# An attention and gated feed-forward kernel whose planner gets a limit on transfers, new margins and a new order of the last output tiles

## The chip, the cores and the metric

The kernel runs on one core of a Trainium2 chip. The metric is device time in microseconds (us), as the median of several executions. Engines are named as the profile names them: PE is TensorE (PEld its weight loads), DVE is VectorE, ACT is ScalarE, POOL is GpSimd, and SP issues most transfers.

## The reference

The first half is attention with a band and a few sink positions, the second a gated feed-forward layer on its result (3072 tokens, width 512, 1536 hidden columns).

```python
scores = (1 / sqrt(64)) * q @ k.T           # 4 batches, 8 heads, 768 positions, 64 wide
keep = (pos_k < n_sink) | ((rel >= 0) & (rel < window))   # n_sink 4, window 128
a = softmax(where(keep, scores, -1e9))
x = (a @ v) as [3072 tokens, 512]
gate = 1 / (1 + exp(-(x @ w_gate)))
out = (gate * (x @ w_val)) @ w_out          # w_gate, w_val: 512 x 1536, w_out: 1536 x 512
```

The three weights come as 64-bit floating-point numbers, which the kernel decodes itself to 32 bits.

## The kernel before

**Order of work.** Nothing is issued where it is written. Every step becomes an operation of a `Plan` (line 254) with a priority, one or several engines it may run on with a duration for each (`ways`), and the tiles that it reads and writes. `Plan.run` then plays the program through once with these durations and writes down, engine by engine, the order in which it would start the operations; that order is what the chip executes. The constants at the top of the file are the planner's durations, margins and due times. `SLACK` and `DSLACK` are added to each hand-over between engines, `SURE` and `SURE_D` are the further time that PE wants an input to be ready for before it prefers the operation (when no operation is that sure, it takes one that is merely ready), `GAP` and `HOLD` let an engine wait for an operation that is due soon, `BACKV` is the queue on DVE from which POOL may take a DVE operation. Where PE has nothing ready in the first 130 us of the plan, `run` inserts matmuls of the identity (`warm`, `m<-ident`), called fills here, if PE was not busy enough in that stretch.

**Attention.** There are 12 pieces of 256 tokens (numbered `tn`), each with 8 heads; `attend` (line 931) plans one head `u` of one piece. PE makes the scores, DVE masks them and finds the maximum (`top`), ACT exponentiates (`exp`), the row sums are inverted, `P` is scaled (POOL, or ACT, or DVE), PE transposes `P`, ACT, DVE and POOL build the masked `wt` from it, and PE multiplies `wt` by the values. The result goes into `xf` (`X0` for the first piece). The first 20 heads (`u < PLAIN`) use plain 32-bit matmuls; later ones split operands in a high and a low part of a faster 32-bit type, whose low part (`rest`) is a subtraction on POOL or DVE.

**Weights.** `decode` (line 1269) turns a 128 x 512 block of a weight into 32 bits in four passes: ACT takes the high word (`ws<-wst`), ACT, DVE or POOL takes the low bits (`wst<-wst`), and DVE shifts and joins (`TENSOR_SCALAR ws<-ws`, `SCALAR_TENSOR_TENSOR ws<-wst,ws`). There are 12 slices `f` of the hidden columns and 36 blocks. `halve` splits a block into high and low parts (`CAST ws<-ws` and a subtraction) and stores the low part to `wlo_d` in device memory; `thirds` forms the combinations that pairs of pieces need.

**Feed-forward.** `CHUNKS` lists the pieces taken together: 0, 1, 2, 3 alone, then four pairs. Per chunk and slice, PE makes the products with the gate and value weights (tiles `m`), ACT takes a tanh, DVE joins both (`SCALAR_TENSOR_TENSOR th<-th...`), ACT rounds to `gh`, DVE or POOL subtracts (`gl<-th,gh`), and PE adds the down products into the output tiles `O` (`o<-...`, `a<-...`). Chunk 0 (`feed_whole`) uses the plain weights; later chunks fetch low parts back from `wlo_d` into 8 `lo` buffers (`fetch`). Priorities of attention come ahead of the products. `out_tiles` (line 1388) halves the finished `O` and stores it; `last_slice` (line 1655) is the last slice of the last chunk.

Of the kernel before, what the change touches and what calls it, by code (L numbers as in the profile page):

```python
# [15 lines left out]
ALU = mybir.AluOpType  # L16
# [13 lines left out]
CROWD = 1.0  # L30
LEAD = 130.0
PWAIT = 100.0
BACKA = 500.0
ALTR = 1.0
BACKV = 300
# [3 lines left out]
GAP = 4.0  # L39
# [3 lines left out]
THIRDS = 140000.0  # L43
CROWDED = 350000.0
PLAIN = 20
SINKP = -3.0
# [5 lines left out]
DR1 = 0.25  # L52
DS2 = 18.0
DR2 = 0.3
KS1 = 16
KR = 1.0
KS2 = 25
# [6 lines left out]
SLACK = 100  # L64
DSLACK = 300
QUEUED = 1000
SHARE = 1.6
ISSUE = 480.0
SURE = 900
SURE_D = 1200  # L70
# [249 lines left out]
class Plan:  # L320
# [39 lines left out]
    def run(self, warm, fill_ns, fill):  # L360
        free, slots, order = {}, {}, []
        events, n = [(0.0, 0, None)], 0
# [26 lines left out]
        port = 0.0  # L389

# [7 lines left out]
        while events:  # L398
            now = events[0][0]
# [25 lines left out]
            for e in free:  # L425
                if free[e] > now:
                    continue
# [6 lines left out]
                while waiting[e] or unsure:  # L434
# [89 lines left out]
                    if o.dma:  # L524
                        dma_free = max(dma_free, now + REACH) + o.dma
                        end = dma_free + LANDED
                    heapq.heappush(events, (end, n, ("end", o, e)))
# [33 lines left out]
def kernel(  # L561
# [74 lines left out]
    def vec(cols):  # L636
        return 80 + 1.0 * cols
# [7 lines left out]
    def act(cols, psum=False):  # L645
        return 28 + 0.93 * cols
# [205 lines left out]
    WLO, SPLIT, GROUPS, DECODED, READY, READY2 = (Fixed(None) for _ in range(6))  # L852
# [415 lines left out]

    def decode(prio, src, whole):
# [22 lines left out]
                )),  # L1292
                ("G", Port(1305.0), lambda: G.tensor_scalar(
# [3 lines left out]
            ],  # L1297
# [51 lines left out]
    def halves(f):  # L1349

        pr = KS1 + KR * f
        gate, value, wout = wraw[f]
        woh = halve(pr, f, 5, (1, DO), wout, (), HALVED)
        gh = halve(pr, f, 3, (NC, 128), gate)
        vh = halve(pr, f, 4, (NC, 128), value)
        wres[f] = [gh, vh, woh]
# [17 lines left out]
    def halved(p, acc, ot):  # L1374

        a, b = (lambda x, i=i: x()[:, i * 256 : i * 256 + 256] for i in range(2))
        plan.op(
            p, [("A", act(256, True), lambda: A.mul(out=a(ot), in_=a(acc), mul=0.5))], [acc],
            [(ot, 0)],
        )  # L1380
        plan.op(
            p, [("V", vec(256), lambda: V.tensor_scalar(
                out=b(ot), in0=b(acc), scalar1=0.5, scalar2=None, op0=ALU.mult
            ))],
            [acc], [(ot, 1)],
        )

    def out_tiles(ci, g, T, O):

        for j, acc in enumerate(O):  # L1390
            last = ci == len(CHUNKS) - 1
            ot = tile([128, DO], F32, *(("xf", BUFS["xf"]) if last else ("w2", BUFS["w2"])))
            r = (g + j) * 128
            ways = [
                ("A", act(DO, True), lambda acc=acc, ot=ot: A.mul(out=ot(), in_=acc(), mul=0.5)),
                (
                    "V", vec(DO), lambda acc=acc, ot=ot: V.tensor_scalar(
                        out=ot(), in0=acc(), scalar1=0.5, scalar2=None, op0=ALU.mult
                    ),
                ),  # L1400
            ]
            if last and j == 1:
                halved(-1000.0 + ci + 1, acc, ot)
            else:
                plan.op(-1000.0 + ci + 1, ways if last else ways[:1], [acc], [ot])
            e, E = ("A", A) if last and j < 2 else ("Q", Q)
            plan.op(
                ci, [(e, ISSUE, lambda E=E, ot=ot, r=r: E.dma_start(out=out[r : r + 128], in_=ot()))],
                [ot], dma=moved(8, 2048),
            )  # L1410
# [251 lines left out]
    def last_slice(pr, pe, O, th, cv, woh, wol):  # L1662
# [3 lines left out]
        for h in (1, 0):  # L1666
# [22 lines left out]
            (2, high), (3, high), (2, small), (3, small), (0, high), (0, small), (1, high), (1, small)  # L1689
        )  # L1690
        for n, (j, (x, ws)) in enumerate(order):

            def down(j=j, x=x, ws=ws):
# [8 lines left out]
                [(x, j // 2), woh, wol], [O[j]],  # L1702
# [138 lines left out]
```

## Time and profile before

| what | value |
|---|---|
| median of 3 runs (lowest to highest) | 762.97 us (762.62 to 764.37) |
| the profiled execution's own time | 759.45 us |
| its span, first to last instruction | 757.7 us |
| PE busy | 746.0 us, 98% |
| DVE, ACT, POOL busy | 619.2, 479.4, 454.5 us |
| granted TensorE clock, mean | 0.998 |
| moved from and to device memory | 159.24 and 25.17 MB |

The span is what the profile divides into shares; the execution's own time is 1.75 us longer. Matmuls are pipelined and their ends are modelled, so a PE shown as busy can still lose some tenths of a microsecond between two matmuls; a plain 32-bit matmul stands in the trace as two records. A wait of the weight load (PEld) can be longer than what PE loses by it, since loads run ahead.

### The profile page before, as it was taken

What the parts mean: (1) busy time and instruction counts of PE and PEld (TensorE: products, weight loads), DVE (VectorE), ACT (ScalarE), POOL (GpSimd) and SP (SyncE); (2) the same over time, 40 slices, a digit from 0 to 9 for tenths busy, and PEclk for the clock granted to TensorE, in tenths of its full rate; (3) what the DMA queues carried; (4) which work ended last, traced back from release to release, by engine and by line L of the source; (5) the groups of instructions that cost most, each with busy time, mean ns of one, the idle gap of its engine ahead of it and who ended that gap; (6) DMA issues with size and microseconds to landing.
All of it is one profiled execution on the core that took longest, in us unless ns stands there. A gap on an engine that the chain in (4) does not pass through costs nothing.

```text
span 757.7 us, 16323 instructions
## 1 busy us (share of the span) xinstructions
PE 746.0 (98%) x5020; PEld 680.0 (90%) x5020; DVE 619.2 (82%) x1796; ACT 479.4 (63%) x1378; POOL 454.5 (60%) x592
## 2 busy tenths in 40 slices
PE   8999999999999999999999999999999999999996
PEld 7888777999899999999999999999999999999995
DVE  6998999899997799899889989889988877544443
ACT  8999997776855577776656776465676642322212
POOL 3857676899995487986665976467766652200000
PEclk9999999999999999999999999999999999999999
DMA  6999999897999976688677677776787655676662
GB/s 196 263 291 287 309 319 334 262 323 233 315 322 312 333 227 207 186 280 258 208 245 227 209 260 247 233 232 215 235 286 214 206 168 185 224 234 210 205 197 98
DMA packets 111661, 185.55 MB, mean 245 GB/s; under 512 B 23248, under 2 KB 32976, under 8 KB 111568
## 3 DMA queue, kind: packets, MB, share of 16 engines
q1 hardware_dynamic: 111280, 183.93, 76.5%
q8 instruction: 41, 0.67, 0.4%
q10 hardware_dynamic: 288, 0.52, 0.2%
q14 instruction: 52, 0.43, 0.2%
HBM read 159.24 MB, written 25.17 MB: 243 GB/s over the span
## 4 chain that ended last, share of the span: by engine, by line
PE 84%; DVE 7%; DMA 3%; ACT 3%; issue 2%; POOL 1%; SPq 0%; DVEq 0%; POOLq 0%; ACTq 0%
PE m L630 45%; PE a L630 22%; PE o L630 16%; DVE ws L630 2%; DMA wst<-in_moe_w_gate_dram 1%; DMA lo<-wlo_d 1%; ACT P L630 1%; DVE P L630 1%; ACT ws L630 1%; DVE xf L630 1%; DVE th L630 0%; DMA qkT<-in_qk_dram 0%; DVE a L630 0%; ACT wst L630 0%; SPq L630 0%
## 5 line engine op out<-in xcount | busy, mean ns | idle before, releaser
L630 PE MATMUL m<-ws,lo 128*128 128x256 f32 x1344 | 289.6, 282 | 0.3 <-DMA lo<-wlo_d 0.2
L630 PE MATMUL m<-ws,ws 128*128 128x256 f32 x1536 | 289.5, 285 | 0.0
L630 PEld LDWEIGHTS m<-ws,ws 128*128 128x128 f32 x1536 | 242.4, 189 | 8.5 <-issue 0.5
L630 PEld LDWEIGHTS m<-ws,lo 128*128 128x128 f32 x1344 | 216.0, 189 | 0.8 <-DMA lo<-wlo_d 0.7
L630 POOL TENSOR_SCALAR_AFFINE_SELECT wt<-wt 128x512 fp32r<-128x512 f32 (+3 forms) x192 | 128.0, 668 | 55.5 <-DVE wt L630 38.3
L630 ACT ACTIVATE P<-P,negm_all 128x144 f32<-128x144 f32 x192 | 78.7, 411 | 33.2 <-DVE negm_all L630 29.9
L630 ACT ACTIVATE th<-m 128x256 f32<-128x256 f32 x96 | 37.2, 387 | 86.0 <-DVE th L630 72.2
L630 ACT CAST gh<-th 128x512 fp32r<-128x512 f32 (+1 forms) x81 | 42.4, 525 | 46.8 <-DVE th L630 46.3
L630 POOL TENSOR_TENSOR kl<-qkT,hi 128x400 fp32r<-128x400 f32 (+1 forms) x60 | 62.2, 1037 | 14.1 <-ACT hi L630 12.0
L630 POOL TENSOR_TENSOR ws<-ws,ws 128x512 fp32r<-128x512 f32 (+1 forms) x51 | 65.4, 1291 | 6.8 <-DVE ws L630 5.6
L630 PE MATMUL o<-ws,gh 128*128 128x512 f32 x168 | 68.0, 405 | 0.0
L630 PE MATMUL o<-ws,gl 128*128 128x512 f32 x168 | 66.1, 393 | 0.2 <-DVE gl L630 0.2
L630 PE MATMUL o<-lo,gh 128*128 128x512 f32 x168 | 65.7, 391 | 0.0
L630 DVE CUSTOM_DVE_ANT_0 P<-a,am 128x144 f32<-128x144 f32 x192 | 58.5, 306 | 7.5 <-PE a L630 1.5
L630 DVE TENSOR_TENSOR gl<-th,gh 128x512 fp32r<-128x512 f32 (+1 forms) x76 | 52.3, 690 | 12.6 <-ACT gh L630 10.7
L630 PE MATMUL a<-wt,vhl 128*128 128x256 f32 (+2 forms) x282 | 60.0, 323 | 0.2
L630 POOL TENSOR_TENSOR P<-P,rs 128x288 f32<-128x288 f32 x47 | 35.0, 746 | 41.9 <-DVE rs L630 36.6
L630 POOL TENSOR_TENSOR hi<-qkT,hi 64x256 fp32r<-64x256 f32 x57 | 45.2, 793 | 18.4 <-issue 5.2
L630 DVE TENSOR_TENSOR cv<-m,cv 128x256 f32<-128x256 f32 x96 | 40.2, 419 | 19.4 <-ACT cv L630 12.2
L630 PEld LDWEIGHTS a<-wt,vhl 128*128 128x128 f32 x282 | 47.9, 189 | 7.8 <-POOL wt L630 1.2
L630 ACT CAST hi<-qkT 128x656 fp32r<-128x656 f32 (+1 forms) x67 | 47.2, 705 | 12.1 <-PE a L630 8.9
L630 DVE COPY_PREDICATED a<-tri,a 128x128 f32<-128x128 int32 x160 | 45.6, 285 | 2.5 <-PE a L630 2.1
(145 smaller groups left out, 1695.2 us busy)
## 6 DMA issues: line engine op xcount, KB each, us to landing
lo<-wlo_d SPq DMA_DIRECT2D x396, 256.0 KB, 3.3
wlo_d<-ws SPq DMA_DIRECT2D x72, 256.0 KB, 4.5
qkT<-in_qk_dram SPq DMA_DIRECT2D x52, 328.0 KB, 4.2
qkT<-in_qk_dram SPq DMA_DIRECT2D x24, 264.0 KB, 4.0
wst<-in_moe_w_gate_dram SPq DMA_DIRECT2D x12, 512.0 KB, 5.2
wst<-in_moe_w_val_dram SPq DMA_DIRECT2D x12, 512.0 KB, 5.2
wst<-in_moe_w_out_dram SPq DMA_DIRECT2D x12, 512.0 KB, 5.5
out_dram<-w SPq DMA_DIRECT2D x20, 256.0 KB, 4.1
```

The source lines that it names most:

```text
L630: return lambda *a, **kw: tc.keep_in_program_order(op(*a, **kw))
```

## The change

`Plan.run` keeps the ends of all planned transfers, and starts no further one on SP while eight (`LANES`) are under way. The low-bit pass of the first 12 decoded blocks (`NOG`) has no POOL way any more. The splits of gate and value blocks may start at 30 us of the plan at the earliest (`HSTART`). Some twenty constants change: the hand-over margins (`SLACK` 100 to 30, `DSLACK` 300 to 150, `SURE` 900 to 300, `SURE_D` 1200 to 1800), `GAP` 4 to 2, `BACKV` 300 to 0 (POOL takes a DVE operation whenever it is free), `PWAIT`, `CROWD`, priorities of splits and decodes. In the last chunk `halved` is gone: tiles 0, 1 and 2 are halved whole by DVE and tile 3 by ACT, three of the four stores are issued by ACT instead of two, and the down products of the last slice finish tile by tile, in an order that a common tile `ENDS` keeps.

```diff
--- before.py
+++ after.py
@@ -27,47 +27,50 @@
 NWS = 68
 WARM = 130000.0
 FLOOR = 0.75
-CROWD = 1.0
+CROWD = 1.02
 LEAD = 130.0
-PWAIT = 100.0
+PWAIT = 50.0
 BACKA = 500.0
 ALTR = 1.0
-BACKV = 300
+BACKV = 0
 FLIP = 1
 HOLD = 0.8
 HELD = 800000.0
-GAP = 4.0
+GAP = 2.0
 LATER = 45000.0
 HALVED = 40000.0
 TSTEP = 8000.0
-THIRDS = 140000.0
+THIRDS = 130000.0
 CROWDED = 350000.0
 PLAIN = 20
-SINKP = -3.0
+SINKP = -2.0
 SCALP = -0.5
 SKSWAP = 0
 WHOLE = 1
 DN1 = 36
 DS1 = 7
-DR1 = 0.25
+DR1 = 0.3
 DS2 = 18.0
 DR2 = 0.3
-KS1 = 16
+KS1 = 15
 KR = 1.0
-KS2 = 25
+KS2 = 23
 XP = -900.0
 ALT = 1
 AFTER = dict(PE=163.0, V=75.0, A=100.0, G=35.0, Q=0.0)
 TOLD = dict(PE=54.0, V=35.0, A=35.0, G=77.0, Q=27.0)
 REACH = 2000.0
 LANDED = 430.0
-SLACK = 100
-DSLACK = 300
+SLACK = 30
+DSLACK = 150
 QUEUED = 1000
 SHARE = 1.6
+HSTART = 30000.0
+NOG = 12
+LANES = 8
 ISSUE = 480.0
-SURE = 900
-SURE_D = 1200
+SURE = 300
+SURE_D = 1800
 FREE = 150.0
 NEXT = dict(PE=0.0, V=10.0, A=25.0, G=0.0, Q=0.0)
 UPS = 2
@@ -387,6 +390,7 @@
         dma_free, window, active, cold = 0.0, 1, [0.0] * 1000, True
         HAM = 4096 / 1.2
         port = 0.0
+        landings = []
 
         def busy(a, b, frac):
             while a < b:
@@ -424,6 +428,10 @@
                         heapq.heappush(events, (x.ready, n, ("ready", x, None)))
             for e in free:
                 if free[e] > now:
+                    continue
+                if e == "Q" and len(landings) >= LANES and landings[-LANES] > now:
+                    n += 1
+                    heapq.heappush(events, (landings[-LANES], n, None))
                     continue
                 if e == "Q" and dma_free > now + REACH + QUEUED:
                     n += 1
@@ -524,6 +532,7 @@
                     if o.dma:
                         dma_free = max(dma_free, now + REACH) + o.dma
                         end = dma_free + LANDED
+                        landings.append(end)
                     heapq.heappush(events, (end, n, ("end", o, e)))
                     for x in o.then:
                         x.before -= 1
@@ -849,7 +858,7 @@
     HALVES, FIRST = {}, []
 
     X0 = {}
-    WLO, SPLIT, GROUPS, DECODED, READY, READY2 = (Fixed(None) for _ in range(6))
+    WLO, SPLIT, GROUPS, DECODED, READY, READY2, ENDS = (Fixed(None) for _ in range(7))
 
     def sinks(b, u):
         if not b:
@@ -1266,6 +1275,8 @@
     wlo_d = dram.tile([NF, 128, 6 * 512], F32, name="wlo_d")
     LAST = [None]
 
+    counted = iter(range(3 * NF))
+
     def decode(prio, src, whole):
 
         n, m = src.shape[1], src.shape[2]
@@ -1290,11 +1301,12 @@
                 ("V", Port(900.0), lambda: V.tensor_scalar(
                     out=by(2), in0=by(1), scalar1=13, scalar2=None, op0=ALU.logical_shift_right
                 )),
+            ] + [
                 ("G", Port(1305.0), lambda: G.tensor_scalar(
                     out=by(2), in0=by(1), scalar1=2.0**-13, scalar2=-8191.0 / 16384, op0=ALU.mult,
                     op1=ALU.add,
                 )),
-            ],
+            ] * (next(counted) >= NOG),
             [], [st],
         )
         plan.op(
@@ -1351,8 +1363,8 @@
         pr = KS1 + KR * f
         gate, value, wout = wraw[f]
         woh = halve(pr, f, 5, (1, DO), wout, (), HALVED)
-        gh = halve(pr, f, 3, (NC, 128), gate)
-        vh = halve(pr, f, 4, (NC, 128), value)
+        gh = halve(pr, f, 3, (NC, 128), gate, (), HSTART)
+        vh = halve(pr, f, 4, (NC, 128), value, (), HSTART)
         wres[f] = [gh, vh, woh]
 
     def thirds(f):
@@ -1371,20 +1383,6 @@
         if f == NF - 1:
             plan.op(pr, [("V", 60, lambda: V.memset(own2, 0.0))], [wres[f][3]], [READY])
 
-    def halved(p, acc, ot):
-
-        a, b = (lambda x, i=i: x()[:, i * 256 : i * 256 + 256] for i in range(2))
-        plan.op(
-            p, [("A", act(256, True), lambda: A.mul(out=a(ot), in_=a(acc), mul=0.5))], [acc],
-            [(ot, 0)],
-        )
-        plan.op(
-            p, [("V", vec(256), lambda: V.tensor_scalar(
-                out=b(ot), in0=b(acc), scalar1=0.5, scalar2=None, op0=ALU.mult
-            ))],
-            [acc], [(ot, 1)],
-        )
-
     def out_tiles(ci, g, T, O):
 
         for j, acc in enumerate(O):
@@ -1399,11 +1397,9 @@
                     ),
                 ),
             ]
-            if last and j == 1:
-                halved(-1000.0 + ci + 1, acc, ot)
-            else:
-                plan.op(-1000.0 + ci + 1, ways if last else ways[:1], [acc], [ot])
-            e, E = ("A", A) if last and j < 2 else ("Q", Q)
+            by = ways[:1] if not last or j == 3 else ways[1:]
+            plan.op(-1000.0 + ci + 1, by, [acc], [ot])
+            e, E = ("A", A) if last and j != 2 else ("Q", Q)
             plan.op(
                 ci, [(e, ISSUE, lambda E=E, ot=ot, r=r: E.dma_start(out=out[r : r + 128], in_=ot()))],
                 [ot], dma=moved(8, 2048),
@@ -1686,7 +1682,7 @@
         high = gh, (lambda: woh()[:, 0], lambda: wol())
         small = gl, (lambda: woh()[:, 0],)
         order = (
-            (2, high), (3, high), (2, small), (3, small), (0, high), (0, small), (1, high), (1, small)
+            (2, high), (2, small), (3, high), (3, small), (0, high), (0, small), (1, high), (1, small)
         )
         for n, (j, (x, ws)) in enumerate(order):
 
@@ -1699,7 +1695,7 @@
 
             plan.op(
                 pe + (1.7 + 0.01 * n) / NF, [("PE", len(ws) * mac(DO), down)],
-                [(x, j // 2), woh, wol], [O[j]],
+                [(x, j // 2), woh, wol], [O[j], ENDS],
             )
 
     def hint(*when):
```

What the plan makes of it, engine by engine: PE has 43 fills before and 33 now, and all its other matmuls are the same in number. DVE has 76 operations fewer (1796 to 1720), POOL 66 more, ACT 28 more. Of the subtractions `gl<-th,gh` POOL has 44 instead of 9; its four low-bit passes go to ACT, and 18 of its 47 scalings of `P` go over to ACT (17, as two instructions each) and DVE (1).

**DVE, up to the copy that completes X0.** This copy (`COPY xf` from tile `a`) is the last of the eight heads of piece 0; the second half of the first slice's products waits for it. Names: `ws` and `wst` are weights being decoded, `am` masks. First before:

```order
L630 COPY sk_129<-a_488 32x128
L630 SCALAR_TENSOR_TENSOR ws_468<-wst_391,ws_468 128x512
L630 COPY_PREDICATED a_508<-tri,a_508 128x128
L630 ISA P_523,negm_all<-a_508,am_89 128x144
L630 ISA negm_all 128x1
L630 RECIPROCAL rs_506<-rs_506 128x2
L630 TENSOR_SCALAR ws_515<-ws_515 128x512
L630 COPY_PREDICATED a_511<-tri,a_511 128x128
L630 ISA P_523,negm_all<-a_511,am_89 128x144
L630 ISA negm_all 128x1
L630 SCALAR_TENSOR_TENSOR ws_515<-wst_424,ws_515 128x512
L630 COPY xf_457<-a_500 128x256
```

and now:

```order
L639 COPY sk_129<-a_467 32x128
L639 CAST ws_476<-ws_244 128x512
L639 SCALAR_TENSOR_TENSOR ws_442<-wst_333,ws_442 128x512
L639 COPY_PREDICATED a_474<-tri,a_474 128x128
L639 ISA P_491,negm_all<-a_474,am_89 128x144
L639 ISA negm_all 128x1
L639 COPY_PREDICATED a_480<-tri,a_480 128x128
L639 ISA P_491,negm_all<-a_480,am_89 128x144
L639 ISA negm_all 128x1
L639 RECIPROCAL rs_463<-rs_463 128x2
L639 TENSOR_SCALAR ws_487<-ws_487 128x512
L639 COPY xf_433<-a_460 128x256
```

Before, the copy stands behind eight joins of decoded blocks (`SCALAR_TENSOR_TENSOR`) counted from the start, now behind five; shifts (`TENSOR_SCALAR ws`) 8 and 6; casts of blocks (`CAST ws`) 2 and 1.

**PE, around the same copy.** `m<-xf` are the products that wait for it, `m<-ident` the fills. Before:

```order
L630 MATMUL a_508<-qkT_103 128x272
L630 MATMUL a_511<-qkT_103 128x272
L630 MATMUL m_91<-ident 128x128 x5
L630 MATMUL a_500<-wt_503,kl_152 128x256
L630 MATMUL a_500<-wt_503,kl_152 128x128
L630 MATMUL a_500<-sk_129,vshl_118 128x128
L630 MATMUL a_500<-sk_129,vshl_123 128x128
L630 MATMUL m_91<-ident 128x128 x3
L630 MATMUL a_557<-ident,P_475 128x128 x2
L630 MATMUL a_557<-ident,P_475 32x128
L630 MATMUL m_91<-xf_457,ws_240 128x256 x2
L630 MATMUL m_92<-xf_457,ws_284 128x256 x2
```

and now:

```order
L639 MATMUL a_474<-qkT_103 128x272
L639 MATMUL a_480<-qkT_103 128x272
L639 MATMUL m_91<-ident 128x128 x4
L639 MATMUL a_460<-wt_478,kl_152 128x256
L639 MATMUL a_460<-wt_478,kl_152 128x128
L639 MATMUL a_460<-sk_129,vshl_118 128x128
L639 MATMUL a_460<-sk_129,vshl_123 128x128
L639 MATMUL m_91<-ident 128x128 x2
L639 MATMUL m_91<-xf_433,ws_244 128x256 x2
L639 MATMUL a_527<-ident,P_451 128x128 x2
L639 MATMUL a_527<-ident,P_451 32x128
L639 MATMUL m_92<-xf_433,ws_292 128x256 x2
```

The last fills stand right ahead of the same products in both; 5 and 3 of them before, 4 and 2 now.

**ACT, at the end.** `xf` are the halved output tiles, `a` and `o` the accumulators. Before:

```order
L630 CAST gh_11359<-th_11323 128x256 x2
L630 ACTIVATE xf_11375<-a_10544 128x512
L630 ACTIVATE xf_11385<-o_10505 128x256
L630 DMA out_dram<-xf_11381 128x512
L630 DMA out_dram<-xf_11385 128x512
```

and now:

```order
L639 CAST gh_11362<-th_11331 128x256 x2
L639 ACTIVATE xf_11383<-a_10552 128x512
L639 DMA out_dram<-xf_11383 128x512
L639 DMA out_dram<-xf_11390 128x512
L639 DMA out_dram<-xf_11393 128x512
```

ACT halves one tile whole and then only issues three stores.

**PE, between the last product of a slice and its first down product.** In the 36 slices of chunks 1 to 3, this stretch of PE's order holds fewer rows now: between the last product that reads the value weight's low part and the first down product with `gh` there were 32 rows in the first of them, 42 in the second and 28 in the third; now there are 26, 17 and 19.

## Rows read from the trace of the kernel before

**Rows 1.** The page, part 1: busy us, share of the span, instructions of each engine.

```profile
PE 746.0 (98%) x5020; PEld 680.0 (90%) x5020; DVE 619.2 (82%) x1796; ACT 479.4 (63%) x1378; POOL 454.5 (60%) x592
```

**Rows 2.** Windows: stretch, its length, busy us of five engines, clock, DMA share, GB/s.

```profile
20.00:40.00 20.00, 19.60 (x125) 17.12 (x124) 18.43 (x53) 19.81 (x55) 16.82 (x20) 1.00 0.99 265
60.00:80.00 20.00, 19.95 (x100) 15.72 (x99) 16.32 (x50) 19.97 (x46) 13.77 (x16) 1.00 0.97 297
...
100.00:130.00 30.00, 29.62 (x142) 22.26 (x140) 28.62 (x74) 25.16 (x65) 20.03 (x25) 1.00 0.96 338
730.00:758.00 28.00, 21.18 (x137) 18.68 (x135) 11.12 (x23) 5.78 (x14) 0.00 (x0) 0.94 0.39 130
```

**Rows 3.** Timeline at 7 to 10 us (start, us, engine, operation): two bursts of fills.

```profile
7.44 1.05 PE L630 MATMUL m<-ident 128*128 128x128 f32 x8
...
9.87 0.39 PE L630 MATMUL m<-ident 128*128 128x128 f32 x2
```

**Rows 4.** Timeline at 35 to 38 us: the copy that completes X0.

```profile
35.78 1.21 DVE L630 SCALAR_TENSOR_TENSOR ws<-wst,ws 128x512 int32<-128x512 int32 x1
...
36.91 0.41 DVE L630 COPY xf<-a 128x256 f32<-128x256 f32 x1
...
37.38 1.16 PEld L630 LDWEIGHTS m<-xf,ws 128*128 128x128 f32 x6 [0.46 <-DVE xf L630]
```

**Rows 5.** Groups on DVE, 0 to 37 us: count, busy us, mean ns, idle before.

```profile
L630 DVE SCALAR_TENSOR_TENSOR ws<-wst,ws 128x512 int32<-128x512 int32 x8 | 6.8, 845 | 0.2
...
L630 DVE TENSOR_SCALAR ws<-ws 128x512 int32<-128x512 int32 x8 | 5.0, 626 | 1.7 <-ACT ws L630 1.7
...
L630 DVE CAST ws<-ws 128x512 fp32r<-128x512 f32 x2 | 1.9, 950 | 0.0
```

**Rows 6.** The same on ACT, 0 to 38.2 us: high-word and low-bit passes, casts.

```profile
L630 ACT ACTIVATE wst<-wst 128x512 uint16<-128x512 uint16 x7 | 9.5, 1357 | 0.0
...
L630 ACT ACTIVATE ws<-wst 128x512 f32<-128x512 f32 x9 | 6.0, 672 | 0.9 <-DMA wst<-in_moe_w_gate_dram 0.9
...
L630 ACT CAST ws<-ws 128x512 fp32r<-128x512 f32 x2 | 1.2, 602 | 0.0
```

**Rows 7.** The chain that ended last: start, us, engine and tile, merged matmuls.

```profile
247.93 1.39 PE o L630 x6
...
662.32 2.87 PE m L630 x24
```

**Rows 8.** Waits of PEld, 130 to 640 us: total us, times, longest.

```profile
PEld o L630 <- DVE gl L630: 1.1, 3, 0.7
PEld m L630 <- DMA lo<-wlo_d: 0.7, 2, 0.4
```

**Rows 9.** Tile lo: transfers from issue to landing.

```profile
DMA to landing us min/median/max: 2.6/3.3/6.1
```

**Rows 10.** Timeline of a slice at 220 to 226 us: DVE, POOL and PE rows.

```profile
223.73 1.28 POOL L630 TENSOR_TENSOR ws<-ws,ws 128x512 fp32r<-128x512 f32 x1
...
224.09 1.21 DVE L630 TENSOR_TENSOR gl<-th,gh 128x256 fp32r<-128x256 f32 x1
...
225.53 0.40 PE L630 MATMUL o<-ws,gl 128*128 128x512 f32 x1
```

**Rows 11.** Timeline of a later slice, 235 to 240 us: its POOL and PE rows.

```profile
237.10 1.18 POOL L630 TENSOR_TENSOR gl<-th,gh 128x256 fp32r<-128x256 f32 x1
...
239.76 0.39 PE L630 MATMUL o<-ws,gl 128*128 128x512 f32 x1
```

**Rows 12.** Tile gl: ns of one, least, median, most; first and last start.

```profile
L630 DVE TENSOR_TENSOR gl<-th,gh x76: 378/691/1292, 133.2 to 748.6; 128x512 fp32r<-128x512 f32 x40, 128x256 fp32r<-128x256 f32 x36
```

**Rows 13.** Timeline from 749 us to the end: the last output tiles.

```profile
749.72 0.69 DVE L630 TENSOR_SCALAR xf<-a 128x512 f32<-128x512 f32 x1 [0.72 <-PE a L630]
...
751.72 0.38 ACT L630 ACTIVATE xf<-o 128x256 f32<-128x256 f32 x1 [1.18 <-DVE xf L630]
751.73 1.44 ACTq L630 DMA_DIRECT2D out_dram<-xf  x2
```

## The prediction

> **What bounds the kernel now.** I read the page first, then the windows, the waits and the chain. The page [rows 1] shows PE busy for 746.0 of 757.7 us: the kernel is bound by PE, and its useful matmuls are the same before and after (only fills change in number). So the change can only move what PE does beside them: fills, waits, the start and the end. The windows [rows 2] show where the 11.7 us of idle PE lie: 0.4 us between 20 and 40 us, 0.05 between 60 and 80, 0.4 between 100 and 130, and 6.5 in the last 27.7 us, where the outputs leave; 4.3 us are left for all other stretches. To this come 43 fills, all ahead of the products that wait for X0. A fill costs 0.22 us: two bursts of 8 and 2 records [rows 3] differ by 0.66 us for six records, 0.11 each, and a fill is two records. So fills take 43 x 0.22 = 9.5 us. After the start PE is full, but so are the engines that feed it: from 20 to 80 us ACT is busy for 19.8 to 19.97 of every 20 us [rows 2].
>
> **The change, part by part.** Sums are made against the profiled execution (759.45 us), and carried over to the median of the runs, which stands 3.5 us higher at 762.97.
>
> *The start.* The copy that completes X0 begins at 36.91 us on DVE, behind a join of 1.21 us, and PE's weight load waits for it for 0.46 us [rows 4]. In the new order DVE has three joins, two shifts and one cast fewer ahead of this copy. With the means of that stretch [rows 5] that is 3 x 0.85 + 2 x 0.63 + 0.95 = 4.8 us; a small copy and a row-sum guard more, some 0.4 us, leave 4.3. DVE is 92% busy there [rows 2], so nearly all of it would show. ACT has, ahead of its first tanh, two high-word passes and two casts fewer, 2 x 0.67 + 2 x 0.60 = 2.5 us [rows 6]. From PE's side the bound is lower: ten fills fewer are 10 x 0.22 = 2.2 us [rows 3]. The lower end is nothing (the copy may be held by ACT or a transfer instead), the upper 4.3. I take **-3.0**, between the fills and DVE and nearest to ACT, the fullest engine of the three.
>
> *Given back up to 130 us.* GpSimd's four low-bit passes all go to ACT, at 1.36 us each [rows 6], 5.4 us in the stretch where ACT has no idle time. In the new order they are spread over the 36 blocks, and ACT is relieved of casts. DVE has 3.7 us idle between 60 and 80 us and ACT 4.8 between 100 and 130 [rows 2], which cover most. If that cover were gone, PE would wait for the tanh of slices 4 and 5, and the gain of the start would go. Bounds 0 and +3.0; I take **+0.7**.
>
> *Eight transfers.* The new order leaves more time between the PE work that frees a `lo` buffer and the first use of its next content: counted in PE's rows, at 0.12 us for a product and 0.23 for a down product [rows 7], the least distance grows from 4.0 to 5.2 us. Landing takes 3.3 us in the median and 6.1 at most [rows 9]. PE's loads waited twice for `lo`, 0.7 us in all [rows 8]. Bounds -0.7 and 0, or a new wait of the same size; I take **-0.4**.
>
> *Thinner margins.* `SURE` falls by 600 ns and `SLACK` by 70 ns for each hand-over, and nothing on the chip becomes faster by that. The same count between the last product of a slice and its first down product gives a median of 4.4 us for the 36 slices of chunks 1 to 3 before, and 3.1 now; 14 of them lie under 3.0, where one did. In this stretch DVE joins, ACT rounds and DVE or POOL subtracts, and PE must find the result ready. How much is left can be read from two slices. In the one at 235 to 240 us POOL ends `gl` at 237.10 + 1.18 = 238.28 and PE reads it at 239.76 [rows 11]: 1.5 us to spare, so 1.3 less still costs nothing. In the one at 220 to 226 us `gl` ends at 225.30 and is read at 225.53 [rows 10]: 0.2 to spare, and with 1.3 less PE would wait for 1.1 us. The attention chains (scores to transposes, transposes to values) lose 1.1 to 1.6 us of the same distance. Only three waits for `gl` were there, 1.1 us [rows 8]. Lower end -0.3 (DVE has 76 operations fewer, chains may shorten by as much); upper end: a third of the 36 slices like the second one, 12 x 1.1 = +13 us. I take **+1.3**, since most chains before had the margin of the first slice and the planner still asks for 0.3 us.
>
> *Subtractions on POOL.* 35 more of the `gl` go to POOL, at 1.18 us [rows 11] instead of a median of 0.69 on DVE [rows 12]. In the pair chunks the distance in PE's order stays at 5.4 us, which covers 0.5 us more: nothing. In the 222 us slice DVE's `gl` took 1.21 us, from 224.09, while POOL worked from 223.73 to 225.01 [rows 10], and the same instruction ranges from 378 to 1292 ns [rows 12]. The Trainium skill ("SBUF — State Buffer", section "SBUF: two separate sides") says that a DVE instruction with two SBUF inputs and a GpSimd instruction exclude each other at a shared pair of ports for the whole instruction. By that rule, on which these rows agree, each subtraction moved to POOL also blocks DVE's; the sum would then be that of the fourth case below.
>
> *The end.* DVE now halves tile 1 whole: 0.69 instead of half a tile [rows 13], about as late as ACT's half ended before (751.72 + 0.38). In exchange ACT has issued its first two stores by then. Before, both of its issues stood behind that half, 1.44 us [rows 13]; now only the last does, 0.4 to 0.9 us. That is 0.5 to 1.0 earlier, less about 0.2 for PE, which asks for the first low product 0.46 us (two down products) sooner than its subtraction was needed. Bounds -0.8 and +0.3; I take **-0.3**. The moved splits and thirds have their readers one chunk or more later; DVE's idle time hides them, and without it they would delay DVE's part of the chains above.
>
> Sum: -3.0 + 0.7 - 0.4 + 1.3 - 0.3 = **-1.7 us**: 757.75 for the profiled execution, **761.3** for the median.
>
> **The rivals.**
> 1. *The start holds* (the sum above). For it: the counts on DVE, ACT and PE point the same way. Alone it spans 757.8 (the start gives 4.3, margins cost little) to 762.
> 2. *No change.* The copy of X0 comes earlier, but ACT and DVE cannot keep the lead, and PE waits for it in slices 3 to 8; or the copy is held by something else and the plan's fewer fills only become idle time. For it: ACT's full windows [rows 2]. The -3.0 and +0.7 become 0, margins and end cancel: 762.97 + 0.6 = **763.5**.
> 3. *Slower by thin margins.* PE waits in many slices and heads between 130 and 640 us. For it: `gl` to spare by only 0.2 us in [rows 10] and the counts. Against it: just two named waits now [rows 8]. It decides from the point where these waits add 3.0 + 1.5 us to today's, four slices like that one; with six of them (6.6 us) the time is 762.97 - 3.0 + 6.6 = **766.6**.
> 4. *Slower by POOL against DVE.* A moved subtraction stretches one on DVE by up to 1.29 - 0.69 = 0.6 us [rows 12]; POOL has 66 operations more. If one in ten lies on a chain that PE waits for, that is 4.0 us, 762.97 - 1.7 + 4.0 = **765.3**.
>
> **How the numbers follow.** The measurement tells 0.2% (1.5 us) from no change. The chances: case 1 0.46, case 2 0.24, case 3 0.22, case 4 0.08. Cases 3 and 4 are the slower 0.30. I take case 1 as the likeliest because its gain is counted in three engines' orders, while the loss of case 3 needs margins whose size I see in two slices. The range reaches from 757.5, the far end of case 1, to 767.0, just over case 3, which leaves out the slices of case 3 beyond it and a start that gains more than DVE's count, together under 2 in 10.
>
> **What would show it.** The copy that completes X0 should start near 33.5 to 34 us, the last fill end before it, and 33 fills stand in the trace. Between 130 and 640 us PEld's waits for `gl`, `P`, `wt` should add under 3 us to today's; if they add over 4.5, case 3 is right. `lo` should wait no more. Joins on DVE that take 1.2 us or more beside POOL, with PE waiting behind them, would show case 4. At the end, ACT's last store should be issued by about 0.5 us sooner after PE's last matmul. I am wrong in the start if the copy stands at 36 us or later.

## The result, and the profile after

The changed kernel takes 767.14 us in the median (765.83 to 769.16, 8 runs) against 763.51 us of the kernel before (761.38 to 765.21, 8 runs): a ratio of 1.0052, 95% interval 1.0034 to 1.0071. It is slower by 3.6 us, more than the 0.2% that a measurement tells. The forecast was 761.3, and it named the wrong case; 767.1 is just beyond the end of the range.

The page of the changed kernel, part 1 (busy us, share of the span of 764.1 us, instructions):

```profile
PE 747.8 (98%) x5000; PEld 677.5 (89%) x5000; DVE 580.3 (76%) x1720; ACT 492.3 (64%) x1405; POOL 515.0 (67%) x658
```

Beside [rows 1], DVE has 39 us less to do and POOL 60 more, and PE is idle for 16.3 us instead of 11.7. The profiled execution of the kernel before (759.45 us) turned out to be quicker than all its other runs, so I took a second profile of it (763.54 us; experiment 9), in which PE is idle for 15.4 us. Idle time alone therefore says little, and the windows must tell where the time goes. The second profile first (stretch, length, then busy us and records of PE, PEld, DVE, ACT and POOL, clock, DMA share, GB/s):

```profile
0.00:130.00 130.00, 122.30 (x628) 98.49 (x629) 109.34 (x327) 118.34 (x280) 77.80 (x110) 1.00 0.92 273
130.00:310.00 180.00, 179.51 (x1281) 167.35 (x1281) 161.12 (x477) 124.89 (x393) 144.93 (x187) 1.00 0.88 284
310.00:330.00 20.00, 19.52 (x142) 18.19 (x140) 16.79 (x49) 15.40 (x46) 19.33 (x26) 1.00 0.66 200
330.00:640.00 310.00, 309.36 (x2185) 288.80 (x2184) 271.41 (x828) 191.69 (x594) 204.37 (x268) 1.00 0.73 229
```

and the same windows of the changed kernel:

```profile
0.00:130.00 130.00, 124.19 (x634) 99.40 (x635) 106.81 (x332) 118.09 (x271) 76.42 (x107) 1.00 0.89 279
130.00:310.00 180.00, 179.73 (x1290) 168.56 (x1289) 160.16 (x488) 130.75 (x402) 165.78 (x212) 1.00 0.88 284
310.00:330.00 20.00, 19.36 (x138) 17.73 (x137) 18.68 (x43) 12.71 (x38) 17.55 (x21) 1.00 0.72 229
330.00:640.00 310.00, 307.07 (x2146) 283.88 (x2146) 246.77 (x754) 201.61 (x630) 232.76 (x304) 1.00 0.72 225
```

The count of PE's records is the number to read: in the same 310 us PE gets through 2146 matmuls instead of 2185. At 309.36 / 2185 = 0.142 us each, 39 fewer are 5.5 us. The first profile of before agrees with the second there: 2184 records in 309.44 us. Between 130 and 310 us, where the chunks of one piece are, the changed kernel has 1290 records and the kernel before 1281 and 1288: nothing is lost there. So the loss lies between 330 and 640 us, in the pair chunks. The waits of PE's weight loads in this stretch, kernel before (second profile; us in total, times, longest):

```profile
PEld a L630 <- issue: 1.3, 4, 0.7
PEld m L630 <- DMA lo<-wlo_d: 0.5, 2, 0.3
PEld o L630 <- DVE gl L630: 0.2, 1, 0.2
```

and the changed kernel:

```profile
PEld a L639 <- issue: 3.4, 8, 0.9
PEld a L639 <- POOL wt L639: 1.6, 5, 0.7
PEld a L639 <- PE a L639: 1.0, 1, 1.0
PEld a L639 <- ACT low L639: 0.7, 1, 0.7
PEld a L639 <- DVE wt L639: 0.4, 1, 0.4
PEld a L639 <- POOL kl L639: 0.4, 1, 0.4
PEld a L639 <- ACT vhl L639: 0.3, 1, 0.3
PEld a L639 <- PE m L639: 0.2, 1, 0.2
```

2.0 us in 7 waits became 8.0 us in 19. All the new ones stand in front of `a`, the tiles of the attention heads; `gl`, which the prediction priced, is gone from the list. Where a row says "issue", the matmul behind the load shows what it waited for (timeline of PEld):

```profile
513.20 0.53 PEld L639 LDWEIGHTS a<-wt,vhl 128*128 128x128 f32 x3 [0.62 <-issue]
```

and of PE:

```profile
513.23 0.70 PE L639 MATMUL a<-wt,vhl 128*128 128x512 f32 x3 [0.44 <-DVE xf L639]
```

PE had to wait until DVE had read an earlier head's result out of an `a` tile. PE's own waits in this stretch, changed kernel:

```profile
PE a L639 <- DVE negm_all L639: 1.5, 3, 0.7
PE a L639 <- DVE xf L639: 0.4, 1, 0.4
PE a L639 <- POOL wt L639: 0.3, 1, 0.3
PE a L639 <- DVE wt L639: 0.3, 1, 0.3
PE a L639 <- POOL kl L639: 0.2, 1, 0.2
```

The row `negm_all` is the end of DVE's search for the maximum, which reads scores out of an `a` tile; the matmuls that waited for it make new scores or a head's result and use no maximum. By that, 1.9 of these 2.7 us are waits for an `a` tile to come free. The kernel before (second profile) has one wait in this list, 0.5 us. The rest of the lost time shows only in the loads' waits above and in wider spacing of the matmuls.

The start did what was forecast. The copy that completes X0, in the kernel before (second profile; timelines of DVE):

```profile
39.58 0.41 DVE L630 COPY xf<-a 128x256 f32<-128x256 f32 x1
```

and in the changed kernel:

```profile
35.27 0.42 DVE L639 COPY xf<-a 128x256 f32<-128x256 f32 x1
```

The 36.91 of [rows 4] belongs to the quick execution.

### The profile page after: what moved, and what is told of

The parts are those of the page before. It is cut to its first block, busy times and chain, and to the rows that moved or that the text cites. A ratio compares the mean times of both kernels' runs of the same rounds, so it can differ in the third digit from the quotient of the medians.

```text
span 764.1 us, 16324 instructions
## 1 busy us (share of the span) xinstructions
PE 747.8 (98%) x5000; PEld 677.5 (89%) x5000; DVE 580.3 (76%) x1720; ACT 492.3 (64%) x1405; POOL 515.0 (67%) x658
## 4 chain that ended last, share of the span: by engine, by line
PE 78%; DVE 8%; ACT 4%; DMA 2%; issue 2%; POOL 1%; SPq 1%; DVEq 0%; ACTq 0%; POOLq 0%
PE m L639 43%; PE a L639 20%; PE o L639 15%; DVE th L639 1%; DVE ws L639 1%; ACT wst L639 1%; DVE xf L639 1%; DMA qkT<-in_qk_dram 1%; DVE cv L639 1%; DMA out_dram<-w 1%; ACT ws L639 1%; ACT th L639 1%; SPq L639 1%; DVE hi L639 1%; DMA lo<-wlo_d 1%
## 5 line engine op out<-in xcount | busy, mean ns | idle before, releaser
L639 PEld LDWEIGHTS m<-ws,ws 128*128 128x128 f32 x1536 | 245.1, 189 | 12.3 <-DVE th L639 0.7
L639 POOL TENSOR_SCALAR_AFFINE_SELECT wt<-wt 128x512 fp32r<-128x512 f32 (+3 forms) x192 | 121.4, 634 | 36.3 <-ACT wt L639 17.0
L639 POOL TENSOR_TENSOR gl<-th,gh 128x512 fp32r<-128x512 f32 (+1 forms) x44 | 51.6, 1172 | 121.8 <-ACT gh L639 113.8
L639 POOL TENSOR_TENSOR ws<-ws,ws 128x512 fp32r<-128x512 f32 (+1 forms) x62 | 77.1, 1253 | 13.8 <-DVE ws L639 12.1
L639 ACT CAST hi<-qkT 128x656 fp32r<-128x656 f32 (+1 forms) x75 | 52.8, 705 | 10.4 <-PE a L639 9.0
L639 PEld LDWEIGHTS a<-wt,vhl 128*128 128x128 f32 x282 | 47.0, 189 | 12.3 <-POOL wt L639 4.5
L639 ACT ACTIVATE P<-P,rs 128x144 f32<-128x144 f32 x126 | 45.4, 409 | 16.2 <-DVE rs L639 15.9
L639 POOL TENSOR_TENSOR hi<-qkT,hi 64x256 fp32r<-64x256 f32 x58 | 47.0, 811 | 9.3 <-POOL wt L639 2.5
L639 ACT ACTIVATE wst<-wst 128x512 uint16<-128x512 uint16 x36 | 48.4, 1360 | 0.1
```

The source lines that it names most:

```text
L639: return lambda *a, **kw: tc.keep_in_program_order(op(*a, **kw))
```

## Experiments

Ratios are medians over those of the kernel before on the same chip, with 95% intervals. Edits are against the changed kernel or the kernel before, as named.

**1. Old margins in the changed kernel.**

```diff
-SLACK = 30
-DSLACK = 150
+SLACK = 100
+DSLACK = 300
-SURE = 300
-SURE_D = 1800
+SURE = 900
+SURE_D = 1200
```

> The changed kernel with the four margins of the kernel before (SURE 900, SURE_D 1200, SLACK 100, DSLACK 300). Theory, thin margins: the 3.6 us are lost in stalls of PE behind P, wt, th, the scores and reused tiles, because PE is planned to use them right after they are ready; with the old margins the ratio to the kernel before falls from 1.005 to 0.999 (0.997 to 1.001), and the waits of PE's weight loads between 130 and 640 us fall from 10.5 to under 6 us. Rival, queues: POOL's larger share (BACKV 0, 35 more gl) slows DVE; the ratio stays at 1.004 to 1.006. Rival, start: the loss is in the new order of decodes and transfers; the ratio stays at 1.003 or more, and the waits between 130 and 640 us hardly matter.

Measured: 0.9986 (0.9967 to 1.0004). As the margins theory had it; POOL's larger share and the new start are still in this kernel.

**2. Thin margins in the kernel before** (the same lines the other way round).

> The kernel before with only the four thin margins (SURE 300, SURE_D 1800, SLACK 30, DSLACK 150). Thin margins: the ratio is 1.004 to 1.008, with waits of PE's weight loads between 130 and 640 us of 9 us or more (4.1 before). Queues or start: the ratio is within 0.999 to 1.002.

Measured: 1.0166 (1.0148 to 1.0183). The direction is the theory's, the size twice what it asked.

**3. Queues as before, in the changed kernel.**

```diff
-BACKV = 0
+BACKV = 300
-GAP = 2.0
+GAP = 4.0
```

> The changed kernel with BACKV 300 and GAP 4 again, so that POOL takes over DVE's work as rarely as before. Queues: the ratio falls to 0.999 to 1.001. Thin margins: it stays at 1.004 to 1.006, as thin hand-overs lose the same whichever engine makes the subtraction.

Measured: 1.0112 (1.0087 to 1.0137). POOL made 3 subtractions `gl` here, fewer than in the kernel before, and the time got no better. By the stage it is no better either: 2136 records of PE between 330 and 640 us, where the changed kernel has 2146. The fourth case of the prediction (POOL against DVE) is not the cause.

**4. A yardstick: the kernel before with one nanosecond more.**

```diff
-SLACK = 100
-DSLACK = 300
+SLACK = 101
+DSLACK = 301
```

> A yardstick: the kernel before with SLACK 101 and DSLACK 301, one nanosecond more at each hand-over, which reshuffles the plan without a reason to be faster or slower. All theories: within 0.998 to 1.002. If it moves by as much as the change did (0.5%), a plan's time is chance at this size, and single constants can't be told apart by one kernel each.

Measured: 1.0033 (1.0019 to 1.0046). One nanosecond reshuffles the whole plan, and that alone is worth 0.3%. From here on a single total could not decide a theory about 0.5%.

**5 and 6. Margins changed from 130 us on.** In `run`, right after `now = events[0][0]`; experiment 5 in the kernel before, as shown, experiment 6 in the changed kernel with the two tuples swapped.

```diff
+            SLACK, DSLACK, SURE, SURE_D = (100, 300, 900, 1200) if now < 130000.0 else (30, 150, 300, 1800)
```

> The kernel before, whose planner takes the four thin margins only from 130 us of the plan on, so that the order of the first 130 us is that of the kernel before. Thin margins in the steady part: ratio 1.005 to 1.010 (thin margins from the start gave 1.0166, of which some 5 us lay ahead of 130 us). Rival, start: all that the thin margins cost lies in the first 130 us, and the ratio is within 0.998 to 1.003.

> The changed kernel, whose planner takes the old margins from 130 us of the plan on; its first 130 us are planned as in the changed kernel. Thin margins in the steady part: ratio 0.998 to 1.001 (the changed kernel has 1.005). Rival, start: 1.004 or more.

Measured: 1.0131 (1.0113 to 1.0149) and 1.0026 (1.0014 to 1.0038). The loss is not in the start. Experiment 6 recovers only half, and its windows show a new place:

```profile
310.00:330.00 20.00, 15.62 (x90) 13.80 (x90) 18.60 (x43) 13.17 (x40) 17.92 (x22) 0.83 0.58 177
```

**7 and 8. Which margin.** The changed kernel with `SURE = 900` and `SURE_D = 1200` alone, and with `SLACK = 100` and `DSLACK = 300` alone.

> The changed kernel with SURE 900 and SURE_D 1200 again, SLACK and DSLACK left thin. If the wish of PE for inputs that are surely there does the work: ratio 0.998 to 1.001. If the hand-over margin does it: 1.004 or more.

> The changed kernel with SLACK 100 and DSLACK 300 again, SURE and SURE_D left as changed. If the hand-over margin does the work: 0.998 to 1.001. If SURE does it: 1.004 or more.

Measured: 0.9962 (0.9947 to 0.9976) and 1.0044 (1.0027 to 1.0061). `SURE` it seems to be, and experiment 7, at 761.65 us, is faster than both kernels.

**9. The kernel before once more, unchanged.**

> The kernel before, unchanged, for a second profile. The profiled execution shown of it took 759.45 us, 4 us less than the median of its other runs. If that execution was a quick one, a second profile shows a span of some 761 to 763 us and the copy that completes X0 at 37.5 us or later (a kernel whose first 130 us are in the same order showed 38.28); the change's start would then have gained some 2 to 3 us after all. If the start of before is steady, the copy stands at 36.9 again and the start gained 1.6 us at most.

Measured: 763.54 us, span 761.8, copy at 39.58 us. The first profile was of a quick execution.

**10, 11 and 12. Reshuffles, and SURE in the kernel before.** Experiment 10 is the changed kernel with `SLACK = 31`, `DSLACK = 151`; 11 is experiment 7 with the same nanosecond; 12 is the kernel before with `SURE = 300`, `SURE_D = 1800`.

> A yardstick for the changed kernel: SLACK 31 and DSLACK 151, one nanosecond more. Thin SURE as the cause: ratio 1.002 to 1.008 around the changed kernel's 1.005. If the 1.005 was the luck of one plan: 1.001 or less.

> The changed kernel with SURE 900 and SURE_D 1200, SLACK 31 and DSLACK 151: the fastest kernel so far, reshuffled. SURE as the cause: 0.994 to 0.999. If its 0.9962 was luck: 1.001 or more.

> The kernel before with SURE 300 and SURE_D 1800 alone. SURE as the cause: 1.005 to 1.015, most of the 1.0166 of all four thin margins. If the hand-over margins do it: 0.999 to 1.003.

Measured: 1.0133 (1.0115 to 1.0150), 1.0094 (1.0074 to 1.0114) and 1.0200 (1.0180 to 1.0220). All three missed their ranges, 10 and 12 on the slow side, as 2, 3, 4 and 5 had before. Experiment 11 missed most: the fastest kernel became 1.3% slower by a nanosecond. Its windows of 320 to 330 us show why:

```profile
320.00:325.00 5.00, 0.58 (x1) 0.28 (x1) 4.97 (x7) 4.75 (x16) 5.00 (x5) 0.50 0.48 126
325.00:330.00 5.00, 4.35 (x19) 4.26 (x20) 4.90 (x7) 1.48 (x5) 4.92 (x7) 0.50 0.00 0
```

and PE's timeline the two waits in them:

```profile
322.94 0.58 PE L639 MATMUL m<-ws,ws 128*128 128x256 f32 x1 [4.16 <-ACT ws L639]
325.65 0.58 PE L639 MATMUL m<-ws,ws 128*128 128x256 f32 x1 [2.13 <-POOL ws L639]
```

Here the first pair of pieces begins, and its inputs (`xf<-xf,xf`, the sum of two pieces, then `ws<-xf`, its high and low parts) are made by ACT, DVE and POOL. ACT's first `CAST ws<-xf` starts at 318.99 us here; in the kernel before, the changed kernel and experiment 7 it starts at 307.87, 306.37 and 304.59. The pieces' last heads come late here, and PE stands for 6.3 us. I call this the border.

**13 to 16. A series in SURE, in the changed kernel:** `SURE` of 0, 600, 900 and 1200, nothing else.

> The changed kernel with SURE 0. So far kernels with SURE 300 lie at ratios of 1.004 to 1.020 and kernels with 900 at 0.996 to 1.009, and a change of one nanosecond moves either by up to 1.3%, so that single pairs can't settle it; a series in SURE on otherwise the same constants can. SURE as the cause: above all kernels with 300 and the same other constants, 1.012 or more. If luck of the plan rules: anywhere between 0.996 and 1.015, without order in SURE.

> The changed kernel with SURE 600. SURE as the cause: between the kernels with 300 and 900, 1.000 to 1.006. Luck: no order in SURE.

> The changed kernel with SURE 900 alone put back; SURE_D stays at 1800. SURE as the cause: 0.995 to 1.001, and less than 20 us lost by PE between 130 and 640 us unless it waits at the border to the pairs at 318 to 326 us, as two of the kernels with 900 did. If SURE_D 1800 costs too: 1.003 or more. Luck: no order in SURE.

> The changed kernel with SURE 1200. SURE as the cause: 0.994 to 1.000, no slower than with 900, as an input that is surer costs only the choice of other work. Luck: no order in SURE. A new wait is possible: PE finds nothing sure and takes what is merely ready; then 1.003 or more.

Measured: 1.0115 (1.0096 to 1.0134), 1.0103 (1.0089 to 1.0116), 1.0096 (1.0079 to 1.0112), 1.0136 (1.0121 to 1.0152). The last three lie above their ranges for `SURE` as the cause. In the totals there is no order in `SURE`: by them, luck would have won. By stages there is. The table has PE's records between 330 and 640 us, the sum of its weight loads' waits there, and PE's busy time between 310 and 330 us; the kernels are sorted by the `SURE` that holds behind 330 us.

| kernel (number of the experiment) | SURE behind 330 us | PE records 330 to 640 us | waits there, us | PE busy 310 to 330 us | ratio |
|---|---|---|---|---|---|
| 13 | 0 | 2128 | 10.3 | 19.04 | 1.0115 |
| after | 300 | 2146 | 8.0 | 19.36 | 1.0052 |
| 2, 3, 5 | 300 | 2106, 2136, 2137 | 12.3, 10.2, 9.0 | 19.78, 19.03, 19.97 | 1.0166, 1.0112, 1.0131 |
| 8, 10, 12 | 300 | 2142, 2114, 2130 | 7.9, 11.5, 10.1 | 17.76, 18.37, 19.20 | 1.0044, 1.0133, 1.0200 |
| 14 | 600 | 2160 | 6.8 | 15.79 | 1.0103 |
| before, 9 | 900 | 2184, 2185 | 1.5, 2.0 | 19.71, 19.52 | 1 |
| 1, 4, 7 | 900 | 2170, 2182, 2173 | 3.1, 2.2, 3.9 | 19.06, 19.83, 19.04 | 0.9986, 1.0033, 0.9962 |
| 6, 11, 15 | 900 | 2196, 2180, 2172 | 0.9, 2.4, 4.3 | 15.62, 13.19, 15.05 | 1.0026, 1.0094, 1.0096 |
| 16 | 1200 | 2166 | 5.5 | 13.94 | 1.0136 |

Every kernel with 300 or less gets through 2106 to 2146 records, every one with 900 or more through 2166 to 2196, and the one with 600 lies between. In this count `SLACK` and `DSLACK` don't matter (8 against after, 7 against 1), nor does `SURE_D` (15 against 7). What hid it is the border: five of the seven changed kernels with 600 or more lose 4 to 7 us there, none with 300 or 0 loses over 2.3, nor does any form of the kernel before. Why a larger `SURE` brings on the late border in the changed kernel alone was not tried.

The order holds for this stage alone. Experiments 2, 5 and 12 have 1245, 1257 and 1236 records of PE between 130 and 310 us, where the kernel before has 1288 and 1281: at 0.14 us each they lose 4 to 7 us more there. But experiment 4, with `SURE` of 900, has only 1260, and all changed kernels lie between 1270 and 1292, whatever their `SURE`. That loss is of these plans; its cause was not tried.

**17 and 18. SURE changed behind the border alone**, on orders that are the same up to there. In `run`, experiment 17 in the changed kernel, as shown; experiment 18 in the kernel before, with 900 and 300 swapped.

```diff
+            SURE = 300 if now < 325000.0 else 900
```

> The changed kernel with SURE 900 from 325 us of the plan on; up to there its order is that of the changed kernel, row for row. Sorted by stage, PE's losses beyond the median spacing of its matmuls were 13.0 to 19.4 us between 330 and 640 us in the eight kernels with SURE 300 or 0 in that stage, and 7.4 to 11.5 us in the eight with 900 or more; five of the changed kernels with 600 or more lost 6 to 8 us more at 310 to 330 us, where the pairs begin. SURE as the cause, with that border as a second thing that hid it: loss between 330 and 640 us 7 to 11.5 us instead of 13.0, none at the border, ratio 0.997 to 1.002. Luck: 13 us or more, ratio 1.004 or more.

> The kernel before with SURE 300 from 325 us of the plan on; up to there its order is that of the kernel before, row for row. SURE as the cause: loss between 330 and 640 us 13 to 19 us instead of 8, ratio 1.006 to 1.015. Luck: 7 to 11 us and a ratio of 0.998 to 1.004.

Measured: 0.9991 (0.9974 to 1.0007) and 1.0070 (1.0049 to 1.0090). The loss that the expectation speaks of is the gap from one matmul's start to the next one's, less the median gap ahead of matmuls of the same tiles and shape in the kernel before; summed from 330 to 640 us it is 9.0 us in experiment 17 and 13.8 in 18. Both ratios and both losses lie in the ranges for `SURE` as the cause. The windows of experiment 17:

```profile
310.00:330.00 20.00, 19.40 (x142) 18.01 (x141) 17.99 (x43) 13.51 (x42) 17.87 (x21) 1.00 0.68 198
330.00:640.00 310.00, 309.06 (x2180) 288.15 (x2180) 256.74 (x788) 194.95 (x605) 241.72 (x315) 1.00 0.73 229
```

and of experiment 18:

```profile
310.00:330.00 20.00, 19.80 (x144) 18.45 (x143) 17.36 (x50) 15.62 (x48) 19.26 (x24) 1.00 0.70 217
330.00:640.00 310.00, 307.20 (x2140) 283.75 (x2139) 267.27 (x818) 193.45 (x602) 207.12 (x263) 1.00 0.72 225
```

and the waits of PE's weight loads in experiment 17, 330 to 640 us, to be held against the eight rows of the changed kernel:

```profile
PEld a L640 <- POOL wt L640: 1.6, 3, 0.7
PEld a L640 <- POOL hi L640: 0.6, 1, 0.6
PEld a L640 <- issue: 0.2, 1, 0.2
PEld a L640 <- POOL kl L640: 0.2, 1, 0.2
```

2146 records become 2180, and 2184 become 2140. In time, 34 x 0.142 = 4.8 us and 44 x 0.142 = 6.2 us; the ratios move by 0.6% (4.7 us) and 0.7% (5.3 us). PE's own waits in experiment 18 are 2.6 us in this stage; 1.2 of them are for `lo`, for which PE has none in the changed kernel. So `SURE` at 300 costs some 5 us in the pair chunks, in both directions. Neither kernel had a reshuffled twin, and kernels of the same `SURE` differ by up to 40 records; what speaks against luck is that the two groups don't overlap in twenty profiles.

## Why the prediction was wrong

**What bounds the kernel**: right. PE is busy for 98%, and the gains and losses that were found are its fills and waits, at a late border also its clock.

**Start, -3.0**: right. Four profiles of the order before have the copy at 36.91, 39.58, 38.28 and 39.66 us (before, 9, 5, 18), three of the order now at 35.27, 35.35 and 35.27 (after, 6, 17): 38.6 less 35.3 is 3.3 us. Against the quick execution from which I counted, the gain is 1.6 us. The absolute time that I named (33.5 to 34) was wrong, as it was counted from one quick execution. Of the 43 fills 33 are left.

**Given back up to 130 us, +0.7**: too small, as far as the profiles tell. Records of PE ahead of 130 us that are no fills (two records for a fill) are 567, 542, 564 and 554 in those four and 568, 568 and 551 in those three. The means differ by 5.6 records; 124 us hold some 560, so that is 1.2 us. Of the 3.3 some 2 are given back. One order alone spreads over 25 or 17 records here, so this is an estimate from few profiles.

**Eight transfers, -0.4**: right in sign. No load waits for `lo` between 130 and 640 us, where 0.7 us were [rows 8] (1.2 in the second profile); one of 0.4 us is left behind 640 us.

**Thinner margins, +1.3**: this is the step that failed. The term measures about 5 us between 330 and 640 us alone (experiments 17, 18). The place in time was that of case 3, which forecast 766.6: the loads' waits between 130 and 640 us rose from 4.1 to 10.6 us, and all of the rise lies behind 330 us. My sign for it, waits for `gl`, `P` and `wt` alone, would have missed it: they rose from 1.3 to 3.3 us, 2.0 more, and I had asked for over 4.5.

I sized the term in the wrong place. The two slices [rows 10, 11] and the 36 distances belong to chunks 1 to 3, whose subtractions `gl` start by 322 us in these profiles; PE lost nothing there. In the pair chunks I saw a distance of 5.4 us that stayed, and put nothing. The attention heads I mentioned and did not price, whereas there the waits came: for `wt` and the low parts, and above all for `a` tiles that DVE had yet to read. The list behind [rows 8] had already shown more than the "two named waits" that I argued with. Besides `gl` and `lo` it holds five groups, 2.3 us, and the longest of all is at `a`:

```profile
PEld a L630 <- issue: 1.3, 4, 0.7
```

I also took `SURE` as a margin for inputs alone. In `Plan.run` (line 455 of the kernel before; there `Plan` begins at 320, `attend` at 905 and `last_slice` at 1662, other than said further up) PE further prefers an operation that needs a new tile only when one has been free for about `SURE`, so with 300 instead of 900 ns the plan counts on `a` tiles that have only just come free. Which of the two uses costs the 5 us was not tried.

And I argued that the planner still asks for 0.3 us. That is a margin against the planner's own durations, and what it has to cover is how far the chip strays from them: of the subtractions in [rows 12], those of one shape, 128x256, alone take 378 to 1292 ns on DVE. That `SURE` pays for this spread fits the waits, but no run shows it. I also lumped four constants; only one of them did it.

**POOL's subtractions, nothing**: right as far as experiment 3 goes. The 0.69 us of DVE that I set against POOL's 1.18 is a median over two shapes; of POOL's 44, 33 are of the wider one, at 1.30 us in the mean.

**End, -0.3**: the size holds in the mean, the way doesn't. From PE's last matmul to the end of the span, seven profiles of the old end have 6.1 to 7.4 us, mean 6.7, and thirteen of the new one 5.6 to 6.7, mean 6.3. But ACT's last store isn't issued sooner. In the changed kernel its three issues stand in one row, which ends at 759.92, 2.1 us behind PE's last matmul (757.77); before, it was 1.9 (means of the seven and the thirteen profiles: 1.7 and 1.9):

```profile
757.06 2.86 ACTq L639 DMA_DIRECT2D out_dram<-xf  x3
```

Where the 0.4 us come from stays open.

**The sum** of what was measured: -1.2 up to 130 us, +5.5 between 330 and 640, -0.4 at the end, +3.9 us; the medians moved by 3.6. **The chances**: case 1 got 0.46 because its gain could be counted in three engines' orders. It could, and it came. The loss was not in what I counted (14 of 36 distances under 3.0 us instead of one), as those slices lost nothing. Case 3, at 0.22, is what happened in size and stage; that its six slices of 1.1 us come out at +3.6 us, as measured, is luck, as no such slice made the loss.

## What to carry to other kernels

Where a planner fixes the order, the margin with which the bound engine prefers sure work has a worth of its own: here 300 instead of 900 ns cost some 5 us in one stage, while five of the seven changed kernels with 600 or more lost as much at the border. Read its worth from many hand-overs, in every stage, on every kind of input and on the buffers that must come free. Before a total of some tenths of a per cent is believed, move the plan by a nanosecond: here that alone was worth 0.3 to 1.3%, and only counts by stage, and orders equal up to one point, told cause from luck. So experiment 7 (0.9962) is the fastest kernel of this study, but its next neighbour, experiment 11, is slower than both kernels: what it shows is a good plan, not good constants.

## What was unexpected of the hardware

**A long wait of PE was paid twice.** In experiment 11 PE stood for 6.3 us at the border, and the granted clock of 320 to 330 us was 0.50, the 1.2 GHz level (windows above). The products behind it ran at half pace:

```profile
326.66 2.98 PE L639 MATMUL m<-ws,lo 128*128 128x256 f32 x13
```

0.23 us each, where 24 took 2.87 [rows 7], 0.12 each. That is some 1.4 us more for these 13. The other four with a late border (6, 14, 15, 16) show a mean clock of 0.83 to 0.91 between 310 and 330 us, all other profiles 1.00.

**The start of one and the same order varies by 2.8 us.** The order up to 130 us of the kernel before gave copies from 36.91 to 39.66 us. In the second profile ACT waited for a weight transfer:

```profile
24.50 0.68 ACT L630 ACTIVATE ws<-wst 128x512 f32<-128x512 f32 x1 [2.30 <-DMA wst<-in_moe_w_val_dram]
```

The changed order, with the limit of eight transfers, held its copy within 0.1 us in three profiles. Whether the limit does that was not tried, and it does not last: up to 130 us the same three have 568, 568 and 551 records of PE.

**Sums on DVE beside POOL.** At the border of experiment 11 two sums on DVE took 1.7 us each while POOL subtracted, and the next one 0.79 beside a shorter operation (timeline of POOL, then of DVE):

```profile
320.15 2.94 POOL L639 TENSOR_TENSOR ws<-xf,ws 128x512 fp32r<-128x512 f32 x2
323.04 0.87 POOL L639 TENSOR_SCALAR_AFFINE_SELECT wt<-wt 128x256 fp32r<-128x256 f32 x1
```

```profile
320.22 3.41 DVE L639 TENSOR_TENSOR xf<-xf,xf 128x512 f32<-128x512 f32 x2
...
323.67 0.79 DVE L639 TENSOR_TENSOR xf<-xf,xf 128x512 f32<-128x512 f32 x1
```

The second sum ends at 323.63 us, 0.54 behind POOL's two subtractions, and the third at 324.46, 0.55 behind POOL's `wt`; in the kernel before the same sum takes 0.69 us at 633.97, where POOL is idle. The Trainium skill ("SBUF — State Buffer", section "SBUF: two separate sides") calls the pair of ports that both share an exclusive lock for a whole instruction; these rows agree. That it lengthens the border was not tried, and by experiment 3 POOL's share did not decide the result.
